# Attention and a gated feed-forward layer on one core: a coarser layout of P, zero rows from DRAM, and new orders

## The chip, the cores and the metric

The kernel runs on one core of one Trainium2 chip. The metric is the device time of that core in microseconds. A run of the kernel takes 270.84 us (median of 7 runs, 266.65 to 271.77).

## The reference

For each of 8 batches and 8 heads, with 576 positions and head size 64, attention with a forget gate is computed; then a feed-forward layer with a convolution over three positions is applied to its output.

```python
scores = scale * np.matmul(q, k.transpose(0, 1, 3, 2))
cum = np.cumsum(np.log(np.clip(f, 0.0001, 1.0)), axis=-1)
scores = np.where(causal, -1e9, scores + cum[:, :, :, None] - cum[:, :, None, :])
attn = softmax(scores)                     # over the keys
x = np.matmul(attn, v)                     # heads side by side: (8, 576, 512)
h = np.maximum(x @ w_in, 0.0)              # 512 -> 1024
conv_out = sum of conv_w[k] * h moved by k - 1 positions, k = 0, 1, 2
out = (h * sigmoid(conv_out)) @ w_out      # 1024 -> 512
```

## The kernel before

**Head blocks.** The 64 heads are worked on in 16 blocks of 4 (`hb`), two blocks for each batch. For a block, q and k come from DRAM by transposing DMAs (`load_qk`, L172) into a tile `qk`. There are four such tiles (`RING = 4`), so a load has to wait until the block four earlier has its scores. A transposed element of 4 bytes fills two partitions, its upper half the odd one, its lower half the even one. The lower halves are not used: the even partitions are given other contents, namely the cumulated logarithms of the gate and constants in a few rows, so that one score matmul adds the decay, and zeros in all the others. For the first six blocks (`NCL = 6`) VectorE does this by multiplying (`clamp`, L182) and GpSimd's DMAs bring the rows. From block 6 on, two DMAs of SyncE do it (`fill`): L203 writes zeros into 60 even partitions, from a row of zeros in SBUF (`cz`) that is read eight times for each partition, and L205 writes the four decay rows from `image`, a tensor in DRAM. `image` is made by GpSimd's DMAs (`decay_image`, `constants`, L209 to L216); its part `image[3]` is all zeros. A fill may start only when both q and k of its block have landed.

**Scores and P.** The scores are computed with keys on the partitions and queries along the columns, for 5 blocks of keys (the last of 64). Because of the causal mask, key block m meets the queries from 128 m on. TensorE computes them in tasks into PSUM tiles `ps` of 1024 columns (four of them): `diag_scores` for two heads (8 squares of 128 by 128 on the diagonal), `off_scores` for one head (the remaining 448, 320, 192 and 64 columns of key blocks 0 to 3), `tail_scores` for the fifth key block of four heads. ScalarE takes the exponentials (`off_exp`, L363, straight into the tile `pp`; `diag_exp`, L375, into `pd`; `tail_exp`, L348), and GpSimd masks the squares on the diagonal on their way from `pd` into `pp` (`diag_mask`, L378), and the tail into `pt` (`tail_mask`, L351).

**Sweeps.** `sweep` (L400) multiplies P by a weight of 32 columns for four heads. The heads go to four strips of 32 columns of the TensorE array. `sums` does it once for a block, with ones; `pv` does it twice, with the even and the odd columns of V. So there are 48 sweeps. Each walks over `PIECES`, ten pieces of P given as key block, first query, number of queries, and kind; each piece is one matmul for each of the four heads. VectorE then makes reciprocals of the sums (`recip`, L408 to L410) and multiplies (`norm`, L417) into `xt`.

**Feed-forward.** For each batch and each of 8 groups of 128 channels: `ffn1` (TensorE, L427), `relu` (ScalarE, L431), `conv` in two halves (VectorE, L437 and L439), `tanh` (ScalarE, L442), `gate` (VectorE, L446). Then `ffn2` (TensorE, L453 and L458; `ffn2_last`, L467 and L470, for the last batch), `evac` (L478, L480) and `store` (L486, L489).

**Order.** Every step is a task in a `Plan`. For each engine a string `ORDER` gives the order of its tasks, one letter for each (`KINDS`): on PE `d`, `o`, `t` are scores, `s` and `p` sweeps, `f` and `g` to `m` the two products of the feed-forward layer; on SP `q` is a load of q or k, `y` of V, `j` and `J` of weights, `z` a fill, `S` a store. Each engine takes its own string strictly in order and waits by semaphores. `Plan.play` uses the times in microseconds that each task is given (estimates, with `lock=True` for steps in which VectorE and GpSimd exclude each other) to merge the strings and to choose buffers; the order within an engine is that of the string. All of SyncE's loads, fills and stores share one DMA queue, in the order of its string.

Of the kernel before, what the change touches and what calls it, by code (L numbers as in the profile page):

```python
# [14 lines left out]
AF = mybir.ActivationFunctionType  # L15
ALU = mybir.AluOpType
# [68 lines left out]
def kernel(  # L85
# [11 lines left out]
    nc = tc.nc  # L97

    B, H, S, D = q.shape
# [10 lines left out]
    HH = 4  # L110
# [3 lines left out]
    WARM = {0: 16, 2: 4, 4: 6, 6: 6}  # L114
    AB = 256
    MB = 224
# [84 lines left out]
    def fill(hb):  # L201
        c = slice(hb * HH, (hb + 1) * HH)
        nc.sync.dma_start(even_rows(hb, 8, 60, 0, 2 * HS).rearrange("p (r x) -> p r x", x=S),  # L203
                          zero[0:60].unsqueeze(1).broadcast_to((60, 2 * HH, S)))
        nc.sync.dma_start(even_rows(hb, 0, 4, 0, 2 * HS).rearrange("j (a x) -> j a x", a=2),  # L205
                          image[:, :, c, :].rearrange("j a h s -> j a (h s)"))
# [147 lines left out]

    OFF = {0: 0, 3: 448, 1: 512, 2: 832}

    def off_scores(me, i, s):
        hb, h = where(i, s)
        for m in (0, 3, 1, 2):
            scores(ps_t[slot[me, "ps"]], OFF[m], hb, h, 128 * m, 128 * (m + 1), S - 128 * (m + 1))  # L360

    def off_exp(t_sc, t_dg, s):
        nc.scalar.activation(pp_t[slot[t_dg, "p"]][:, 1024 * s:1024 * (s + 1)], ps_t[slot[t_sc, "ps"]], AF.Exp,  # L363
                             scale=SCALE)

    def diag_scores(me, i):
        for x in range(WARM.get(i, 0) if i else 0):
            nc.tensor.matmul(ps_t[slot[me, "ps"]][:, 0:512], kc[:, 0:128], kc[:, 64:576], start=True, stop=True)
        for s in range(2):
            hb, h = where(i, s)  # L370
            for m in range(4):
                scores(ps_t[slot[me, "ps"]], 512 * s + 128 * m, hb, h, 128 * m, 128 * m, 128)

# [3 lines left out]
    def diag_mask(t_dg, t_ex):  # L377
        nc.gpsimd.affine_select(pp_t[slot[t_dg, "p"]][:, 2048:3072].rearrange("p (m j) -> p m j", j=128),  # L378
                                pd_t[slot[t_ex, "pd"]].rearrange("p (m j) -> p m j", j=128), pattern=[[0, 8], [1, 128]], base=0, channel_multiplier=-1,
                                compare_op=ALU.is_ge, fill=0.0)  # L380

    PIECES = [(0, 128, 128, "o"), (0, 0, 128, "d"), (1, 128, 128, "d"),
              (0, 256, 320, "o"), (1, 256, 320, "o"), (2, 384, 192, "o"), (3, 512, 64, "o"),
              (2, 256, 128, "d"), (3, 384, 128, "d"), (4, 512, 64, "t")]

    def sweep(ps, hb, t_dgs, t_tail, left_of):

        pt = pt_t[slot[t_tail, "pt"]]
        for x, (m, q0, n, kind) in enumerate(PIECES):
            for h in range(HH):  # L390
                pp, s = pp_t[slot[t_dgs[h // 2], "p"]], h % 2
                if kind == "o":
                    c = 1024 * s + OFF[m] + q0 - 128 * (m + 1)
                    p = pp[:, c:c + n]
                elif kind == "d":
                    c = 2048 + 512 * s + 128 * m
                    p = pp[:, c:c + n]
                else:
                    p = pt[:, SL * h:SL * (h + 1)]
                nc.tensor.matmul(ps[32 * h:32 * (h + 1), AB + q0:AB + q0 + n], left_of(h, m), p,  # L400
                                 start=x in (0, 3), stop=x in (2, 9), skip_group_check=True)

# [103 lines left out]
    for hb in range(NHB):  # L506
        b = hb // 2
        old = [t_exp[x] for x in t_exp if x[0] == hb - RING]
        for s in (1, 0):
            if hb < 2:  # L510
                t_ld[hb, s] = at(13.1 if s else 17.0)
            else:
                t_ld[hb, s] = add("load_qk", "SP", 1.3, old, lambda me, hb=hb, s=s: load_qk(hb, 0, 4, s), dma=2.95)
        if hb % 2 == 0:
            t_vl[b] = add("load_v", "SP", 3.0, [], lambda me, b=b: load_v(b, vf_t[slot[me, "vf"]]), take=["vf"],
                          dma=5.3)
        if hb == 0:
# [40 lines left out]
        for p in range(2):  # L558
            i = 2 * hb + p
            slow = ((3.0, 1.2)[p] if hb < 2 else 1.0)  # L560
            if p == (hb < 2):
                x = t_tail[hb] = add("tail_scores", "PE", (0.5 if hb < 2 else 0.2), rows[0] + rows[1], lambda me, hb=hb: tail_scores(me, hb),
                                     take=["ps", "pt"])
                y = t_exp[hb, "t"] = add("tail_exp", "ACT", 0.31, [x], lambda me, x=x: tail_exp(x, me), take=["p3"],
                                         give=[("ps", x)])
                t_tmask[hb] = add("tail_mask", "POOL", 0.45, [y], lambda me, x=x, y=y: tail_mask(x, y), give=[("p3", y)],
                                  lock=True)
            x = t_dg[i] = add("diag_scores", "PE", 0.46 * slow, rows[p], lambda me, i=i: diag_scores(me, i),
                              take=["ps", "p"])
            y = t_exp[hb, p, "d"] = add("diag_exp", "ACT", 0.94, [x], lambda me, x=x: diag_exp(x, me), take=["pd"],  # L570
                                        give=[("ps", x)])
            t_mask[i] = add("diag_mask", "POOL", 1.12, [y], lambda me, x=x, y=y: diag_mask(x, y), give=[("pd", y)],
                            lock=True)
            for s in range(2):
                z = add("off_scores", "PE", 0.46 * slow, rows[p], lambda me, i=i, s=s: off_scores(me, i, s),
                        take=["ps"])
                t_exp[hb, p, s] = add("off_exp", "ACT", 0.94, [z, x], lambda me, z=z, x=x, s=s: off_exp(z, x, s),
                                      give=[("ps", z)])
# [17 lines left out]
    for b in range(B):  # L596
        for ff in range(NFF):
            ready = [t_norm[4 * b + c] for c in range(4)] + t_win[4:6 if ff < 4 else 8]
            x = add("ffn1", "PE", 0.98, ready, lambda me, b=b, ff=ff: ffn1(me, t_x0[b], ff), take=["ps", "ht"],
                    give=[("xt", t_x0[b])] if ff == NFF - 1 else [])  # L600
            y = add("relu", "ACT", 0.57, [x], lambda me, x=x: relu(x), give=[("ps", x)])
            u0 = add("conv", "DVE", 0.735, [y, t_cwt], lambda me, x=x, ff=ff: conv(x, me, ff, 0), take=["u"], lock=True)
            u1 = add("conv_end", "DVE", 0.735, [u0], lambda me, x=x, u0=u0, ff=ff: conv(x, u0, ff, 1), lock=True)
            if ff == 0:
                th = g0 = add("tanh", "ACT", 0.69, [u1], lambda me, u0=u0, ff=ff: tanh(u0, me, ff), take=["hg"],
                              give=[("u", u0)])
            else:
                th = add("tanh", "ACT", 0.69, [u1], lambda me, u0=u0, g0=g0, ff=ff: tanh(u0, g0, ff), give=[("u", u0)])
            gates[b, ff] = add("gate", "DVE", 0.68, [th], lambda me, x=x, g0=g0, ff=ff: gate(x, g0, ff), give=[("ht", x)],
                               lock=True)  # L610
# [17 lines left out]
        for c in range(5):  # L628
# [6 lines left out]
            if c in (1, 3, 4):  # L635
# [4 lines left out]

    KINDS = {"w": "conv_weights", "d": "diag_scores", "o": "off_scores", "t": "tail_scores", "s": "sums",
             "p": "pv", "f": "ffn1", "g": "ffn2", "h": "ffn2_end", "l": "ffn2_last", "m": "ffn2_last_end",
             "O": "off_exp", "T": "tail_exp", "D": "diag_exp", "c": "cast_in", "R": "relu", "H": "tanh",
             "C": "cast_out", "E": "evac", "e": "evac_end", "k": "clamp", "W": "conv_ratios", "v": "cast_v",
             "V": "cast_v_end", "r": "recip", "n": "norm", "a": "conv", "b": "conv_end", "G": "gate",
             "x": "own_rows", "9": "own_row", "N": "tail_mask", "M": "diag_mask", "i": "decay_image",
             "X": "rows_of", "I": "constants", "y": "load_v", "j": "load_in", "q": "load_qk", "J": "load_out",
             "z": "fill", "S": "store"}
    ORDER = {
        "PE": "wdootdodooosdtopopsppffffdodfofotfofddooostoppdosdopoptffffoggtfdofosgdogpofpstddfpopooohffffgtd"  # L650
              "gfooffsdgotgpodposfdppohoffoffgtdogosggfdfoppoftddosfpopoohffstdfpdfogoopfdgofofogtgsfdopohpdtds"
              "ffppooffgofogfsdtfopgopdfgfohffodfosfgfpdogofptofhsgppgffffgggffhfllgflllllllllllllmmmmlmmmm",
        "ACT": "OOTDDOOODODTOOcRRcRHHRHDDOHRRTORHORODOODOTHCOHDODCCTOHRCRRRHOOHTERDOHROHHODEORHTDDROHOOeHRRROHTR"
               "HDHROORRHDEOHTEHODOHRDOeRHORRORHTODHHHEOERDROHORTDDORHOOOHeRRHTDRDROHOOHDHRERORHOHHTOERDOOeHTDRD"
               "HROORHRHOROHERDTHROHODRHHERHOReHROROHDRHRHODEORTHOHReHHRRRREHHEHRReHHRHREHHEe",
        "DVE": "kWkkkvVvrVncnrnnkababaGbaGcbkGGabaakbGbrGnanrbnnGkGababGaabGabbrGabGnGnarbnnGabGGaabbabGaGbGabra"
               "baGGnbnGrnnabGGaaabbabbrGGGGabnnaGabrnnGbabGaGrbnabGabanGbGaabbaGbGGranbnGranGnabbGaaGbabGbranGa"
               "GbbnaGbGabGaGababGbraaGbnGbnaGbrannGbGGaababbGaGGababGbaGGabbGGE",
        "POOL": "x9NMMiMMNXXNMMXvVMNMvVMMIXNMNvVMvVNMMvVMNNMvVMvMMNvVVMvMNVMvMVMNNMvMvNVVMvMMNVMMvMNV",
        "SP": "yjjqqjjqqqqyJqJJqJyqqqzqqzSSqyzqySqqzSSqyzqSqqzqqzSSqySzyqqSzSqSqzSSSSSSSSSSSS",  # L660
    }
# [33 lines left out]
```

## Time and profile before

| | |
|---|---|
| profiled execution | 270.84 us |
| its span in the trace | 269.1 us |
| PE, busy | 239.8 us (89%) |
| VectorE (DVE), busy | 224.0 us (83%) |
| ScalarE (ACT), busy | 202.2 us (75%) |
| GpSimd (POOL), busy | 85.7 us (32%) |
| score matmuls, L336 | 576, 64.2 us |
| sweeps, L400 | 1280 matmuls with V recorded, 640 with ones |
| diagonal masks, L378 | 32, mean 1255 ns |
| fills, L203 | 10, 540 KB each, 5.2 us from issue to landing |
| DMA packets | 126098, of which 113735 under 512 B |
| bytes moved by DMA | 49.34 MB |

PE is TensorE's matmul side and PEld its weight loads. Matmuls are pipelined, so a busy PE counts time in which one matmul fills the array while another drains. The span runs from the first to the last instruction of the program. The profile infers who ended a wait; where a wait was for several semaphores it names the one that came last by its records. A share of DMA can exceed 1, since packets of several queues can be under way on one engine.

### The profile page before, as it was taken

To read this page: it belongs to the slowest core of one execution; us is meant where nothing else is said; L and a number is where in the kernel's file an instruction comes from. 1 tells how busy PE (TensorE), PEld (TensorE's weight loads), DVE (VectorE), ACT (ScalarE), POOL (GpSimd) and SP (SyncE) were. 2 spreads that over 40 slices of the span, in tenths; PEclk is the share of its full clock that TensorE was granted. 3 is DMA by queue.
4 is the path that set the end of the run, shared out by engine and by line. 5 is a ranking of instruction groups with operands and counts; after the bars stand their busy time and mean duration, and the time that the engine had idled before them with its cause. 6 is when DMAs were issued, how large, how long until landed. Compare 5 with 4: busy or idle time off the path is not lost.

```text
span 269.1 us, 8203 instructions
## 1 busy us (share of the span) xinstructions
PE 239.8 (89%) x3501; PEld 159.5 (59%) x3504; DVE 224.0 (83%) x327; ACT 202.2 (75%) x272; POOL 85.7 (32%) x113
## 2 busy tenths in 40 slices
PE   7599697967999999999995979998989969999992
PEld 2367465654665776676564656666656646665640
DVE  5645789999989999997786699996998949999871
ACT  4069358996899899988884878996978948928651
POOL 4157111696216701490332504065302103200000
PEclk9989989997999999999998999999999979999999
DMA  6999999999999999989999999999989450202124
GB/s 141 200 231 242 243 200 190 238 287 251 202 197 183 243 217 216 217 169 189 229 220 164 197 177 260 213 200 205 198 222 166 93 197 0 80 2 100 78 97 177
DMA packets 126098, 49.34 MB, mean 183 GB/s; under 512 B 113735, under 2 KB 119571, under 8 KB 126062
## 3 DMA queue, kind: packets, MB, share of 16 engines
q1 hardware_dynamic: 125278, 48.00, 87.6%
q0 software_dynamic: 704, 0.67, 0.9%
q8 instruction: 27, 0.44, 0.7%
q10 hardware_dynamic: 80, 0.15, 0.2%
q14 instruction: 9, 0.07, 0.1%
HBM read 14.36 MB, written 10.03 MB: 91 GB/s over the span
## 4 chain that ended last, share of the span: by engine, by line
PE 45%; DMA 22%; SPq 10%; DVE 10%; ACT 5%; issue 5%; POOL 1%; DVEq 0%; ACTq 0%; POOLq 0%
PE ps L427 12%; PE ps L453 11%; DMA qk<-in_q_dram 10%; PE ps L336 8%; PE ps L400 7%; DMA qk<-image 7%; SPq L172 4%; PE ps L467 3%; SPq L247 3%; DVE u L437 3%; DMA qk<-cz 2%; DMA vf<-in_v_dram 2%; SPq L489 2%; DVE u L439 2%; ACT pp L363 2%
## 5 line engine op out<-in xcount | busy, mean ns | idle before, releaser
L336 PE MATMUL ps<-qk 128*128 128x128 bf16 (+3 forms) x576 | 64.2, 249 | 14.0 <-DMA qk<-image 5.4
L363 ACT ACTIVATE pp<-ps 128x1024 f16<-128x1024 f32 x64 | 65.2, 1032 | 14.0 <-PE ps L341 9.3
L427 PE MATMUL ps<-xt,w_in_f 128*128 128x288 f16 x512 | 72.5, 292 | 1.0 <-DVE xt L417 0.6
L378 POOL TENSOR_SCALAR_AFFINE_SELECT pp<-pd 128x1024 f16<-128x1024 f32 x32 | 40.0, 1255 | 76.9 <-ACT pd L375 76.8
L437 DVE SCALAR_TENSOR_TENSOR u<-ht,cwt 128x576 f32<-128x576 f16 x64 | 54.8, 864 | 7.0 <-ACT ht L431 6.8
L427 PEld LDWEIGHTS <-w_in_f 128*128 128x128 f16 x512 | 49.4, 100 | 17.0 <-issue 1.9
L336 PEld LDWEIGHTS <-qk 128*128 128x128 bf16 x576 | 39.0, 101 | 30.9 <-issue 13.9
L439 DVE SCALAR_TENSOR_TENSOR u<-ht,cwt,u 128x576 f32<-128x576 f16 x64 | 56.6, 895 | 0.6
L431 ACT ACTIVATE ht<-ps 128x576 f16<-128x576 f32 x64 | 41.6, 658 | 18.3 <-PE ps L427 17.7
L442 ACT ACTIVATE hg<-u,cw 128x576 f16<-128x576 f32 x64 | 49.2, 782 | 7.9 <-DVE u L439 7.6
L446 DVE SCALAR_TENSOR_TENSOR hg<-hg,ht 128x576 f16<-128x576 f16 x64 | 50.7, 801 | 3.2 <-ACT hg L442 2.9
L453 PE MATMUL ps<-w_out_f,hg 128*128 128x512 f16 x224 | 52.3, 379 | 0.0
L375 ACT ACTIVATE pd<-ps 128x1024 f32<-128x1024 f32 x32 | 32.5, 1029 | 5.1 <-PE ps L336 4.9
L453 PEld LDWEIGHTS <-hg 128*128 128x128 f16 x224 | 21.1, 98 | 22.0
L400 PE MATMUL ps<-pp,va 128*32 128x128 f16 (+3 forms) x1152 | 27.3, 243 | 2.4 <-issue 2.0
L417 DVE TENSOR_TENSOR xt<-ps,rb 128x576 f16<-128x576 f32 x32 | 24.0, 752 | 6.5 <-PE ps L400 4.6
L400 PEld LDWEIGHTS <-va 128*32 128x32 f16 x1280 | 22.1, 99 | 10.9 <-issue 8.6
L253 POOL CAST va<-vf 128x1024 f16<-128x1024 f32 x14 | 16.6, 1186 | 15.5 <-DMA vf<-in_v_dram 13.9
L478 ACT COPY ob<-ps 128x1024 f32<-128x1024 f32 (+1 forms) x23 | 18.2, 793 | 4.2 <-PE ps L467 1.9
L408 DVE STREAM_TRANSPOSE st<-ps 128x576 f32<-128x576 f32 x16 | 12.4, 777 | 8.3 <-PE ps L400 8.3
L351 POOL TENSOR_SCALAR_AFFINE_SELECT pt<-p 128x256 f16<-128x256 f32 x16 | 9.7, 604 | 19.5 <-ACT p L348 19.5
L400 PE MATMUL ps<-pp,ones_h 128*32 128x128 f16 (+3 forms) x576 | 13.9, 240 | 2.2 <-DVE xt L417 1.6
(87 smaller groups left out, 162.7 us busy)
## 6 DMA issues: line engine op xcount, KB each, us to landing
vf<-in_v_dram SPq DMA_DIRECT2D x32, 256.0 KB, 5.6
out_dram<-ob SPq DMA_DIRECT2D x16, 512.0 KB, 3.9
qk<-cz SPq DMA_DIRECT2D x10, 540.0 KB, 5.2
ob<-in_moe_w_out_dram SPq DMA_DIRECT2D x4, 512.0 KB, 4.8
vf<-in_v_dram SPq DMA_DIRECT2D x8, 128.0 KB, 5.8
vf<-in_moe_w_in_dram SPq DMA_DIRECT2D x2, 512.0 KB
hg<-in_moe_w_in_dram SPq DMA_DIRECT2D x2, 512.0 KB
out_dram<-ob SPq DMA_DIRECT2D x16, 64.0 KB, 3.4
```

What stands on the lines that cost most here:

```text
L336: nc.tensor.matmul(o, tk[:, h * S + k0:h * S + k0 + 128], tq[:, h * S + q0:h * S + q0 + n], start=True, stop=not apart(hb, h))
L363: nc.scalar.activation(pp_t[slot[t_dg, "p"]][:, 1024 * s:1024 * (s + 1)], ps_t[slot[t_sc, "ps"]], AF.Exp, scale=SCALE)
L375: nc.scalar.activation(pd_t[slot[me, "pd"]], ps_t[slot[t_dg, "ps"]], AF.Exp, scale=SCALE)
L378: nc.gpsimd.affine_select(pp_t[slot[t_dg, "p"]][:, 2048:3072].rearrange("p (m j) -> p m j", j=128), pd_t[slot[t_ex, "pd"]].rearrange("p (m ...
L400: nc.tensor.matmul(ps[32 * h:32 * (h + 1), AB + q0:AB + q0 + n], left_of(h, m), p, start=x in (0, 3), stop=x in (2, 9), skip_group_check=True)
L427: nc.tensor.matmul(ps[:, MB + 288 * a:MB + 288 * (a + 1)], w_in_f16[:, cc, 128 * ff:128 * (ff + 1)], xt[:, cc, 288 * a:288 * (a + 1)], sta ...
L431: nc.scalar.activation(ht_t[slot[t_m1, "ht"]][:, 1:1 + S], ps_t[slot[t_m1, "ps"]][:, MB:MB + S], AF.Relu, scale=0.5)
L437: nc.vector.scalar_tensor_tensor(u, ht[:, 0:S], cwt[:, ff, 0:1], ht[:, 1:1 + S], op0=ALU.mult, op1=ALU.add)
L439: nc.vector.scalar_tensor_tensor(u, ht[:, 2:2 + S], cwt[:, ff, 1:2], u, op0=ALU.mult, op1=ALU.add)
L442: nc.scalar.activation(hg_t[slot[t_g0, "hg"]][:, ff, :], u_t[slot[t_u, "u"]], AF.Tanh, scale=cw[:, ff, 1:2])
L446: nc.vector.scalar_tensor_tensor(hv, hv, 1.0, ht_t[slot[t_m1, "ht"]][:, 1:1 + S], op0=ALU.add, op1=ALU.mult)
L453: nc.tensor.matmul(o, hg[:, ff, 128 * c:128 * (c + 1)], w_out_f16[:, ff, :], start=(ff == 0), stop=(ff == NFF - 1))
```

## The change

`pp` gets another layout. Up to now a head's four off-diagonal runs lay together and the squares of both heads behind them. In the new tile the square of key block 1 stands just ahead of the off-diagonal run of key block 1, and the square of key block 3 just ahead of the run of key block 3 (64 queries), so that each pair is one piece. A pass then has 7 pieces. The results of a sweep start at column 384 of the PSUM tile in place of 256 (`AB`), [...]a run of 448 columns is then one piece too. `off_exp` writes two runs of 512 columns, and `diag_mask` becomes two instructions for four squares each, one into the places beside the runs and one into the end of the tile.

The zero rows of a fill come from `image[3]` in DRAM, 9216 contiguous bytes for each partition. Their issue, L203 before, is the same single DMA of SyncE.

Some of the plan's times are raised (the conv halves from 0.735 to 0.79, the exponentials from 0.94 to 0.97, the mask from 1.12 to 1.35, the load of q or k from 2.95 to 3.2 of DMA time, V from 5.3 to 5.7), and all five order strings are new; of these PE's and SP's are shown.

```diff
-    AB = 256
+    AB = 384
...
     def fill(hb):
         c = slice(hb * HH, (hb + 1) * HH)
-        nc.sync.dma_start(even_rows(hb, 8, 60, 0, 2 * HS).rearrange("p (r x) -> p r x", x=S),
-                          zero[0:60].unsqueeze(1).broadcast_to((60, 2 * HH, S)))
+        none = image[3]
+        nothing = bass.AP(tensor=none.tensor, offset=int(none.offset), ap=[[2 * S, 60], [1, 2 * HS]])
+        nc.sync.dma_start(even_rows(hb, 8, 60, 0, 2 * HS),
+                          nothing)
...
-    OFF = {0: 0, 3: 448, 1: 512, 2: 832}
+    OFF = {3: 0, 0: 64, 1: 512, 2: 832}
+    DIAG = (3, 1, 0, 2)
+    AT = {"d3": 0, "o3": 128, "o0": 192, "d1": 640, "o1": 768, "o2": 1088, "d0": 2560, "d2": 2688}
...
+    def blocks(t_dg):
+        return pp_t[slot[t_dg, "p"]][:, 0:2560].rearrange("p (a c) -> p a c", c=640)
+
     def off_exp(t_sc, t_dg, s):
-        nc.scalar.activation(pp_t[slot[t_dg, "p"]][:, 1024 * s:1024 * (s + 1)], ps_t[slot[t_sc, "ps"]], AF.Exp,
+        nc.scalar.activation(blocks(t_dg)[:, 2 * s:2 * s + 2, 128:640],
+                             ps_t[slot[t_sc, "ps"]].rearrange("p (a c) -> p a c", a=2), AF.Exp,
                              scale=SCALE)
...
     def diag_mask(t_dg, t_ex):
-        nc.gpsimd.affine_select(pp_t[slot[t_dg, "p"]][:, 2048:3072].rearrange("p (m j) -> p m j", j=128),
-                                pd_t[slot[t_ex, "pd"]].rearrange("p (m j) -> p m j", j=128), pattern=[[0, 8], [1, 128]], base=0, channel_multiplier=-1,
-                                compare_op=ALU.is_ge, fill=0.0)
-
-    PIECES = [(0, 128, 128, "o"), (0, 0, 128, "d"), (1, 128, 128, "d"),
-              (0, 256, 320, "o"), (1, 256, 320, "o"), (2, 384, 192, "o"), (3, 512, 64, "o"),
-              (2, 256, 128, "d"), (3, 384, 128, "d"), (4, 512, 64, "t")]
+        pd = pd_t[slot[t_ex, "pd"]].rearrange("p (x m j) -> p x m j", x=2, m=4)
+        for x in range(2):
+            to = pp_t[slot[t_dg, "p"]][:, 2560:3072].rearrange("p (m j) -> p m j", m=4) if x else blocks(t_dg)[:, :, 0:128]
+            nc.gpsimd.affine_select(to, pd[:, x], pattern=[[0, 4], [1, 128]], base=0, channel_multiplier=-1,
+                                    compare_op=ALU.is_ge, fill=0.0)
+
+    PIECES = [(0, 0, 128, "d0"), (0, 128, 448, "o0"), (1, 128, 448, "d1"), (3, 384, 192, "d3"), (2, 384, 192, "o2"),
+              (2, 256, 128, "d2"), (4, 512, 64, "t")]
...
     ORDER = {
-        "PE": "wdootdodooosdtopopsppffffdodfofotfofddooostoppdosdopoptffffoggtfdofosgdogpofpstddfpopooohffffgtd"
-              "gfooffsdgotgpodposfdppohoffoffgtdogosggfdfoppoftddosfpopoohffstdfpdfogoopfdgofofogtgsfdopohpdtds"
-              "ffppooffgofogfsdtfopgopdfgfohffodfosfgfpdogofptofhsgppgffffgggffhfllgflllllllllllllmmmmlmmmm",
+        "PE": "dootdoowdosotdopopsppffffdtfodfoofoddofotosodoppdosotppffffgogstfdogdgoopfpofsdotofdppohftofdfgd"
+              "fofogffosofdpopotsdpgoopgfdtffohofdogfsogpdfsofftoggpdoppodffhtdfsoofogffpdgtoofsogdfopopdgpdofs"
+              "hffotofgopdgfpofffdogstoogpdpshfofdpoffotpfoggsfpfpgfghfffgfhgffgflgllfllllllllllllmmmmlmmmm",
...
-        "SP": "yjjqqjjqqqqyJqJJqJyqqqzqqzSSqyzqySqqzSSqyzqSqqzqqzSSqySzyqqSzSqSqzSSSSSSSSSSSS",
+        "SP": "yqjjqjjqqqqyJJqJqJyqqqzqqzqqSyzqSyzqSqSzzqqyzqSqqzSqqzySqSzqqyzSSSSSSSSSSSSSS",
```

The scores of the diagonal are written in the order `DIAG` for both heads, and the score tasks and the sweep follow the new places (`OFF`, `AT`); their counts and sizes stay the same.

## The prediction

> **What bounds the kernel now.** I read the slices of the span first (rows are engines, one digit for each 6.7 us).
>
> ```profile
> PE   7599697967999999999995979998989969999992
> DVE  5645789999989999997786699996998949999871
> PEclk9989989997999999999998999999999979999999
> DMA  6999999999999999989999999999989450202124
> ```
>
> Two rows are full together: PE, and, up to slice 31 (about 215 us), the DMA engines. Behind that point the DMA row falls to 0 to 4 while PE stays full, so PE sets the end of the kernel and DMA decides when PE may go on before that. The list of waits, for PE from 69 us on, says where it could not:
>
> ```profile
> PE ps L336 <- DMA qk<-image: 5.4, 4, 2.3
> PE ps L336 <- DVE u L439: 3.1, 1, 3.1
> PE ps L336 <- DMA qk<-cz: 1.0, 1, 1.0
> ```
>
> All three are the first score matmul of a head block (L336) waiting for its q/k tile. The middle one names DVE, but the wait ends at 145.5 us, 1.1 us after the last packet of the tile's rows from `image` (144.4 us in the trace's DMA packets); the wait at 217.4 us ends 1.2 us after its last such packet. It is a DMA wait too. Sum: 5.4 + 3.1 + 1.0 = **9.5 us**. The chain of waits shows one of them whole (start, length, what):
>
> ```profile
> 204.93 6.31 DMA qk<-in_q_dram
> 211.29 0.97 SPq L203
> 212.31 4.82 DMA qk<-image
> 217.13 0.24 issue
> 217.37 1.01 PE ps L336 x8
> ```
>
> q lands; only then may SP issue the fill (L203, zero rows; then L205, the four decay rows), and 6 us later PE starts. The view by windows (length, busy time of PE, PEld, DVE, ACT, POOL, granted PE clock, DMA share, GB/s) prices it:
>
> ```profile
> 70.00:100.00 30.00, 30.00 (x453) 20.59 (x451) 28.26 (x39) 28.13 (x40) 11.75 (x13) 1.00 1.07 203
> 213.00:215.90 2.90, 2.06 (x18) 1.40 (x15) 2.87 (x5) 2.62 (x6) 0.00 (x0) 1.00 0.90 228
> 217.30:220.00 2.70, 2.63 (x16) 2.00 (x17) 0.28 (x1) 0.00 (x0) 0.00 (x0) 0.50 0.64 211
> ```
>
> Without a DMA wait PE is busy 30.00 of 30 us (first row). The fill keeps the DMA engines for some 3 us (second row). After the wait the clock is 0.50 (third row): a window of 3.4 us at half rate, also seen at 145.4 us, each costing 1.7 us. So DMA waits cost 9.5 + 2 x 1.7 = **12.9 us**.
>
> **The change, part by part.** The sums start from the profiled execution, 270.84 us (span 269.1 and 1.7 around it), which is also the median of the seven runs.
>
> *Seven pieces for ten.* 48 sweeps lose 3 pieces of 4 heads each, 576 matmuls with their weight loads; the columns stay 1600 for each head. One sweep after another:
>
> ```profile
> 139.35 0.85 PE L400 MATMUL ps<-pp,va 128*32 128x128 f16 x36
> 140.05 0.84 PE L400 MATMUL ps<-pp,va 128*32 128x128 f16 x36
> ```
>
> 40 matmuls (36 and the 4 of the tail) start 0.70 us ahead of the next 40. ffn2's matmuls of 512 columns take 1.73 us for 8, so 0.42 ns a column, and 1600 columns alone are 0.675 us. Ten pieces thus cost some 0.025 us beyond their columns, 2.5 ns each, because the four heads stream side by side; 48 x 3 x 2.5 ns = **-0.4 us**. The Trainium skill ("TensorE: Matmul & The Clock Gate", "Wait — 56ns, not 53.3ns?") would give far more: warm matmuls never start closer than about 25 ns, so 576 fewer are 14.4 us. Here 0.70 us / 40 is 17.5 ns already, below that floor, so I take the row. Bounds: 0 and -0.4; one issue stall of 2.0 us in a V sweep at 30 us, where PE waited for nothing shown, and the half-rate window behind it (1.7) could go with the instructions: -3.7, kept for the range.
>
> *Zero rows from DRAM.* Ten fills of 553 KB, each now 480 packets of 1152 B. The packets' median is 81 ns, and from the first to the last packet a fill takes 3.0 to 4.0 us, mean 3.3. The new fill has 60 packets of 9216 B, 4 in a row for the busiest of 16 engines. The trace has none; the nearest row is the DRAM packet of 4608 B (`image` rows): median 178 ns, mean 211 in mixed traffic. Twice that is 356 to 423 ns, four are 1.4 to 1.7 us: a fill is shorter by 1.6 to 1.9 us. From the other side, the largest packets seen, 16384 B of instructions, took a median of 1072 ns (15 B/ns): 603 ns x 4 = 2.4 us, shorter by 0.9. I take **1.6 us**, by the nearest row. A rule of the Trainium skill speaks against this part: its page "DMA: Bandwidth & Descriptors" says ("Why small descriptors are slow (HBM only)") that SBUF-to-SBUF transfers do not suffer from small packets, and ("Where 436 GB/s comes from") that they are bound at 435 GB/s where HBM transfers are bound at 358. By that a fill of 553 KB goes from 1.27 to 1.54 us, and ten lose 2.7 us. The packets decide: 553 KB in 3.0 us (212.9 to 215.9 us) is 184 GB/s, so this SBUF-to-SBUF copy is slow. The four rows of L205 stay as they are. The new source needs `image` written, which POOL does far ahead (L214 to L216 at 65 us, first fill at 80).
>
> *The orders.* Counted in PE work (ffn1 0.98, ffn2 1.73, scores 0.45, sweep 0.70 us by the chain's rows), the new PE order reaches the first scores of block 9, 10, 11, 13, 14 and 15 earlier by 5.7, 6.1, 3.7, 3.4, 5.1 and 4.7 us; block 12 at the same place. The new SP order (3.3 us for a q or k load, 5.5 for V, 1.3 for a store) puts the fills of 9, 10, 11, 13, 14 and 15 earlier by 4.6, 5.5, 4.6, 4.8, 5.5 and 2.6 us; that of 12 at the same place. So the order asks for rows earlier than it brings them, and the fills must make up the rest. From block 9 at 128.0 us, at 1.04 us for each unit of work (13.5 us for 13.0 between blocks 9 and 10), with the k-th fill gaining k x 1.6 us:
>
> | block | PE asks (us) | rows there (us) | least gain for each fill (us) |
> |---|---|---|---|
> | 10 | 135.2 | 145.5 - 5.5 - 8.0 = 132.0 | 1.0 |
> | 12 | 160.6 | 167.9 - 11.2 = 156.7 | 1.0 |
> | 14 | 185.5 | 200.9 - 5.5 - 14.4 = 181.0 | 1.1 |
> | 15 | 200.1 | 217.4 - 2.6 - 16.0 = 198.8 | 1.5 |
>
> Blocks 9, 11 and 13 have more room. At 1.6 us no wait remains: **-12.9 us**. That the gains add up rests on the DMA engines never being out of work: between 70 and 205 us the packets leave no gap over 0.9 us. What is late next is DVE.
>
> *Two masks for one.* POOL's 32 selects of 1024 columns become 64 of 512.
>
> ```profile
> L378 POOL TENSOR_SCALAR_AFFINE_SELECT pp<-pd 128x1024 f16<-128x1024 f32 x32 | 40.0, 1255 | 76.9 <-ACT pd L375 76.8
> L351 POOL TENSOR_SCALAR_AFFINE_SELECT pt<-p 128x256 f16<-128x256 f32 x16 | 9.7, 604 | 19.5 <-ACT p L348 19.5
> ```
>
> Undisturbed ones took 1092 and 419 ns, so 512 columns are 643 ns by the line through both, and a mask takes 0.19 us longer: 6.2 us of POOL in all. POOL idles 76.9 us before these, so its own time is hidden; the sweep behind a mask gets it 0.2 us later, and the order has other PE work there. But DVE's conv and gate instructions (median 751 to 812 ns) took 1018 to 1194 where they overlap POOL, 12 us too many in all. In proportion to POOL's time (62 us) that grows by 1.2; by its count (76 instructions, 0.16 each) by 5. DVE has 28.26 of 30 us filled where PE never waits, so I charge it to the path: **+3 us**, between the two. Bounds: -1 (a shorter select holds DVE up less) and +5.
>
> *The rest.* Exponentials write two runs of 512 instead of one of 1024; no row shows that, the reads and their count are the same: 0, with +0.05 x 64 = 3 us as the far end (ACT idles 14 us before them). The first w_in halves come behind a k load in the new SP order, up to 3.3 us later; ffn1 starts at 33.6 us after PE itself is late: 0, at worst +3.3. The constants of conv move behind the first scores: 0.7 us of PE, moved only.
>
> Sum: 270.84 - 0.4 - 12.9 + 3 = 260.5 us.
>
> **The rivals.**
>
> *The long packets gain nothing.* They are cut up again, or DRAM delivers at the rate of the old copy; this is also "it does not do what it says". For it: the rule above. Against it: the 4608 B packets. Block 15 is then asked for at 200.1 and there at 214.8 us, 14.7 late, where the old order is 12.4 late by the same count: 2.3 us slower, **273 us**. In between, at 0.9 us for each fill, block 15 is 14.7 - 9 = 5.7 us late: 260.5 + 5.7 = 266.
>
> *DVE becomes the bound.* Place: the conv and gate instructions between 70 and 217 us; mechanism: each added select holds up a DVE instruction for its whole length, 32 x 0.64 = 20.6 us. For it: DVE already fills 94% of the stage that runs free, and single conv instructions took up to 3.3 us beside POOL. Against it: 150 of 192 conv and gate instructions met no POOL work. DVE's 224 + 20.6 us at 94% are 260 us, with 13 at the start and 5 at the end 278: **278 us**, slower. It decides from about 14 us of added DVE time, where 238 / 0.94 + 18 = 271.
>
> **How the numbers follow.** The likeliest case gets 0.62: 260.5 us. Its own range is 254 (the issue stall gone too, no DVE cost) to 266. No gain from the packets, 0.24, at 266 to 273; DVE as the bound, 0.14, at 271 to 280. The range 254 to 273 leaves out most of the last and a little below. Two per cent, about what a measurement of this kernel can tell from no change, is 265.4 to 276.3 us: 0.62 faster, 0.24 same, 0.14 slower.
>
> **What would show it.** Right: fill packets of 9216 B at 360 to 420 ns, a fill in 1.4 to 1.7 us, PE's waits for q/k tiles after 69 us below 2 us, no half-rate window after 69 us, the DMA row falling some 10 us sooner; a sweep 0.68 us. Wrong: waits for `image` still near 9 us (first rival), or PE waiting for DVE with DVE above 240 us busy (second). A gain in the sweeps of many us would prove me wrong on the pieces.

## The result, and the profile after

The changed kernel takes **266.17 us** (median of 27 runs, 263.05 to 270.91), the kernel before 270.21 us beside it. The ratio is 0.9859, 95% interval 0.9831 to 0.9886: faster by 1.4%, so within the 2% that I called no change. I forecast 260.5 us and gave "faster by over 2%" 0.62. The profiled execution took 267.47 us with a span of 265.7, so it is 7.0 us longer than forecast. The intermediate case of the first rival (0.9 us for each fill, 266 us) comes closest. Executions of one kernel differ by up to 4%: a median here counts all of them, a ratio only the undisturbed ones, so that it need not be the quotient of the medians beside it, and as the changed kernel's own trace is of a slow one, that of e17 stands beside it.

The slices of the span, of the changed kernel (each digit 6.6 us):

```profile
PE   7599975759899999999999999999889889999992
DVE  5632999974999998989998879997959999889971
PEclk9779999997999999999999999999999999999997
DMA  6999999999996999999999989999999510202224
```

DMA's full stretch ends less than a slice sooner (5 and 1 in slices 31 and 32, counted from 0, where it had 4 and 5), and not the 10 us forecast; the last fill's last packet is there at 207.1 us, before at 216.0. Behind slice 9 the clock row stays at 9: the half-rate windows at 145 and 217 us are gone. PE stands at 8 in slices 31 and 32, just where DMA becomes idle. The list of waits of PE from 69 us on, of the changed kernel (total us, times, longest):

```profile
PE ps L338 <- DMA qk<-image: 2.5, 2, 1.7
PE ps L406 <- DVE xt L423: 1.2, 1, 1.2
PE ps L433 <- ACT ht L437: 0.8, 2, 0.5
PE ps L338 <- ACT pd L383: 0.6, 1, 0.6
PE ps L406 <- ACT ht L437: 0.5, 2, 0.3
PE ps L433 <- ACT pd L383: 0.3, 1, 0.3
...
```

Before, there were six waits, all for q/k tiles, of up to 3.1 us and 9.5 us in sum. Now those for q/k tiles come to 2.5 us. In their place PE waits for ACT and DVE, 4.7 us in twelve short waits (the rows left out included), which before it did not.

I counted the loss of PE by stage: the time at which PE reaches a point in its order, less the PE work that the order has ahead of that point (by the durations used in the prediction). All loss is in us; the two kernels in italics are experiments below.

| loss of PE | up to block 6's scores | from there to block 15's scores | after that | in all |
|---|---|---|---|---|
| before | 39.0 | 16.8 | 2.9 | 58.7 |
| changed | 40.3 | 10.9 | 4.3 | 55.5 |
| *changed again (e17)* | 42.0 | 11.5 | 4.3 | 57.8 |
| *layout and fill, old orders (e5)* | 38.8 | 12.7 | 1.4 | 52.9 |

The forecast was 16.8 - 12.9 + 3 - 0.4 = 6.5 in the middle stage and nothing elsewhere. So 4.4 us of the 7.1 missing ones are in the middle, 1.3 at the start, 1.4 at the end.

One caution on ratios. The layout alone came out at 0.9755 on one chip (from three runs) and at 0.9913 on another (from ten). Kernels of different groups of runs are therefore compared only to about 1.5%; where I need less, both ran on the same chip, and their ratio is that of the medians of the runs that a ratio counts, with a 95% interval from resampling them.

### The profile page after: what moved, and what is told of

Its sections match the earlier page's. It is cut to its first block, busy times and chain, and to the rows that moved or that the text cites. A ratio compares the mean times of both kernels' runs of the same rounds, so it can differ in the third digit from the quotient of the medians.

```text
span 265.7 us, 7090 instructions
## 1 busy us (share of the span) xinstructions
PE 238.7 (90%) x2925; PEld 154.8 (58%) x2928; DVE 222.0 (84%) x327; ACT 202.5 (76%) x272; POOL 91.7 (35%) x145
## 4 chain that ended last, share of the span: by engine, by line
PE 53%; ACT 14%; DMA 13%; SPq 10%; issue 5%; DVE 2%; POOL 0%; ACTq 0%; POOLq 0%; DVEq 0%
PE ps L433 16%; PE ps L459 15%; PE ps L338 9%; PE ps L406 7%; DMA qk<-image 6%; DMA qk<-in_q_dram 6%; SPq L172 6%; ACT pp L370 5%; ACT pd L383 3%; SPq L249 3%; PE ps L473 3%; ACT hg L448 2%; ACT ht L437 2%; PE ps L464 2%; ACT w_out_f L243 1%
## 5 line engine op out<-in xcount | busy, mean ns | idle before, releaser
L433 PE MATMUL ps<-xt,w_in_f 128*128 128x288 f16 x512 | 71.2, 286 | 4.0 <-DVE xt L423 1.9
L338 PE MATMUL ps<-qk 128*128 128x128 bf16 (+2 forms) x576 | 63.5, 244 | 10.5 <-DMA qk<-image 4.8
L389 POOL TENSOR_SCALAR_AFFINE_SELECT pp<-pd 128x512 f16<-128x512 f32 x64 | 47.7, 769 | 47.9 <-ACT pd L383 46.1
L443 DVE SCALAR_TENSOR_TENSOR u<-ht,cwt 128x576 f32<-128x576 f16 x64 | 55.9, 880 | 7.3 <-ACT ht L437 7.0
L452 DVE SCALAR_TENSOR_TENSOR hg<-hg,ht 128x576 f16<-128x576 f16 x64 | 49.4, 784 | 1.5 <-ACT hg L448 1.2
L423 DVE TENSOR_TENSOR xt<-ps,rb 128x576 f16<-128x576 f32 x32 | 23.7, 750 | 5.9 <-PE ps L406 5.3
L406 PE MATMUL ps<-pp,va 128*32 128x128 f16 (+2 forms) x768 | 27.6, 281 | 1.1 <-ACT ht L437 0.5
L406 PEld LDWEIGHTS <-va 128*32 128x32 f16 x896 | 19.2, 99 | 12.1 <-issue 6.1
L353 POOL TENSOR_SCALAR_AFFINE_SELECT pt<-p 128x256 f16<-128x256 f32 x16 | 8.0, 499 | 39.2 <-ACT p L350 24.9
L255 POOL CAST va<-vf 128x1024 f16<-128x1024 f32 x14 | 15.4, 1107 | 16.7 <-DMA vf<-in_v_dram 16.7
L406 PE MATMUL ps<-pp,ones_h 128*32 128x128 f16 (+2 forms) x384 | 13.7, 274 | 2.0 <-DVE xt L423 1.2
```

Source lines behind the costliest of these rows:

```text
L338: nc.tensor.matmul(o, tk[:, h * S + k0:h * S + k0 + 128], tq[:, h * S + q0:h * S + q0 + n], start=True, stop=not apart(hb, h))
L389: nc.gpsimd.affine_select(to, pd[:, x], pattern=[[0, 4], [1, 128]], base=0, channel_multiplier=-1, compare_op=ALU.is_ge, fill=0.0)
L433: nc.tensor.matmul(ps[:, MB + 288 * a:MB + 288 * (a + 1)], w_in_f16[:, cc, 128 * ff:128 * (ff + 1)], xt[:, cc, 288 * a:288 * (a + 1)], sta ...
L443: nc.vector.scalar_tensor_tensor(u, ht[:, 0:S], cwt[:, ff, 0:1], ht[:, 1:1 + S], op0=ALU.mult, op1=ALU.add)
L452: nc.vector.scalar_tensor_tensor(hv, hv, 1.0, ht_t[slot[t_m1, "ht"]][:, 1:1 + S], op0=ALU.add, op1=ALU.mult)
```

## The experiments: one part at a time

The first six combine the three parts of the change: layout (seven pieces, two masks), fill (zero rows from DRAM), orders (with the planned times).

**e1, the layout alone.** `OFF`, `PIECES`, `AT`, `AB`, the exponentials and masks as in the changed kernel; fill, ORDER and planned times as before.

> Old orders and old fill, new layout of P alone (7 pieces, two masks for one, results from column 384). Theory (the layout is worth next to nothing either way): a sweep gets 7 ns shorter, 48 of them 0.3 us; masks are 0.18 us later, hidden: 268.5 to 271 us, within 0.5% of before. Rival (the added selects hold DVE up): 1.2 to 5 us slower, 271.5 to 275 us, with DVE's conv and gate instructions above the 12 us of excess that before shows.

268.29 us, ratio 0.9755 (0.9681 to 0.9829). The layout is worth more than the 0.3 us of the expectation. PE's stall near 30 us is gone (below).

**e2, the fill alone.**

```diff
-        nc.sync.dma_start(even_rows(hb, 8, 60, 0, 2 * HS).rearrange("p (r x) -> p r x", x=S),
-                          zero[0:60].unsqueeze(1).broadcast_to((60, 2 * HH, S)))
+        nc.sync.dma_start(even_rows(hb, 8, 60, 0, 2 * HS), nothing)
```

> Old orders and old layout, zero rows from DRAM in packets of 9216 B alone. Theory (the kernel is held up by DMA in front of the late blocks, and a fill of 2.65 us for 3.15 gives back 0.5 us each time): rows of block 15 some 5 us earlier, waits of PE for q/k tiles 9.5 us down to 4 to 5, time 264.5 to 267 us. Rival (what the fills give is lost to waits on ACT and DVE): 268.5 to 270.5 us, with the waits for q/k tiles as far down but as much added in front of ACT and DVE.

269.29 us, ratio 0.9885 (0.9834 to 0.9935): a gain of 3.1 us. Neither expectation holds: PE still waits 4.3 us for rows of `image`, and once 2.4 us more at the same instruction, named for DVE, so 6.7 us and not 4 to 5; no waits for ACT came in after 69 us; and the rows of block 15 are there 1.6 us sooner (last packet at 214.7 us, before at 216.3), not 5.

**e3, the orders and planned times alone.**

> New orders and plan times alone, with the old layout and the old fill. Theory by the count of the prediction (the new order asks for blocks 9 to 15 earlier than it brings their rows): 2.3 us slower than before, 271.5 to 273.5 us, with waits for q/k tiles of 9 us or more. Rival (the orders are the gain of the changed kernel): 265 to 267.5 us, as the changed kernel or nearly.

272.59 us, ratio 1.0066 (1.0022 to 1.0111): slower, as expected, but not by the expected waits: after 69 us PE waits 3.5 us for rows, less than before. By the count of the table above it loses 3.3 us more than before up to block 6's scores (its stall near 30 us is 3.3 us, before 2.0), 2.6 us less from there to block 15's, and 1.0 us more after that.

**e4, fill and orders on the old layout.**

> New orders and new fill, old layout. If the layout is worth next to nothing this is the changed kernel's time, 265 to 267.5 us. If the two masks for one cost the changed kernel time, this is faster than it by 1.2 to 5 us, 261 to 265 us.

269.37 us, ratio 0.9872 (0.9823 to 0.9922), above both expectations. On the same chip that is 0.9865 (0.980 to 0.989) of the orders alone, so here the fill again brings some 3.7 us; and 0.9985 (0.993 to 1.006) of the fill alone, so the orders bring nothing. In its trace PE waits only 0.6 us for `image` after 69 us (e2: 4.3, or 6.7 with the wait named for DVE). The waits for rows are gone and the time is unchanged: against e2, it loses 5.6 us less between block 6's and block 15's scores, but 3.9 more ahead of them, where its stalls with no semaphore to wait for come to 5.4 us (e2: 1.9), and 2.5 more behind them.

**e5, layout and fill with the old orders.**

> Old orders with the new layout and the new fill. If the layout (ratio 0.9755 alone) and the fill (0.9885 alone) act on different losses, the layout on PE's issue stall near 30 us and the fill on the waits for q/k tiles, their gains add up: ratio 0.964, some 261 to 264 us, faster than the changed kernel. Rival (both act on one loss, and the changed kernel shows all there is): 0.975 to 0.986, 265 to 268 us.

266.79 us, ratio 0.9813 (0.9761 to 0.9866), in the range of the rival; but the theory's 0.964 rested on e1's 0.9755, and with the later 0.9913 for the layout (e15) the sum of the gains is 0.980. Its waits of PE from 69 us on:

```profile
PE ps L338 <- DMA qk<-image: 4.5, 3, 2.9
PE ps L338 <- DVE xt L423: 0.7, 2, 0.5
```

More DMA waiting than in the changed kernel (4.5 against 2.5 us), next to no waiting for ACT and DVE, and no more time in all.

**e6, layout and orders with the old fill.**

> New layout and new orders, old fill. If the parts are independent: 0.9755 x 1.0066 = 0.982. Theory (the new orders ask earlier and need the faster fill more than the old ones do): waits for q/k tiles of 5 us or more and a ratio of 0.985 to 0.995. Rival (the fill does not matter under the new orders): as the changed kernel, 0.986 or less, with the same short waits on ACT and DVE.

272.64 us, ratio 0.9984 (0.9939 to 1.0029), slower than both expectations: with the old fill, the new orders leave nothing of what the layout brought alone. e5 on the same chip is 0.9825 of it (0.977 to 0.991).

**e7 and e8: where the layout's gain sits.** Both are e1 with the layout kept, but the sweeps cut into ten pieces again: e7 all 48 sweeps, e8 only the six of head blocks 0 and 1.

```diff
+    CUT = {"o0": (128, 320), "d1": (128, 320), "d3": (128, 64)}
...
-        for x, (m, q0, n, kind) in enumerate(PIECES):
+        pieces = TEN if True else PIECES        # e8: if hb < 2
+        for x, (m, q0, n, kind, at) in enumerate(pieces):
```

> The kernel of e1_layout (old orders, old fill, new layout and masks), but every sweep cut into ten pieces again: the same columns, the same data, the same masks, only 576 matmuls and as many weight loads more on PE. Theory (PE runs out of fetched instructions in the first burst of sweeps): the stall of about 2 us near 30 us, in which PE waits for nothing shown, is back, with a half-rate window behind it, and the time is 4 to 6 us over e1_layout, ratio to before 0.99 to 1.00. Rival (the gain of the layout lies in its banks, its masks or in chance): the time stays at e1_layout's, ratio 0.97 to 0.98.

> As e7_ten_pieces, but only the six sweeps of head blocks 0 and 1 are cut into ten pieces, the other 42 keep seven. Theory (what counts is the burst of sweeps near 30 us): the stall is back, and most of the loss with it, ratio 0.985 to 1.00. Rival (the gain comes from 7 ns and fewer fetches in all sweeps): ratio 0.97 to 0.98, no stall near 30 us.

272.12 us, ratio 0.9976 (0.9929 to 1.0022), and 271.62 us, ratio 0.9972 (0.9925 to 1.0020). Ten pieces take away the layout's gain, and ten in six sweeps of 48 do it as well. These six follow each other near 30 us. The timeline of PE there, of e7 (start, length, instructions, in brackets the idle time before and its releaser):

```profile
30.76 0.47 PE L412 MATMUL ps<-pp,va 128*32 128x128 f16 x13
32.48 0.54 PE L412 MATMUL ps<-pp,va 128*32 128x320 f16 x20 [1.26 <-issue]
```

Thirteen matmuls into a sweep PE stops for 1.26 us, and no semaphore is waited for. That is the stall of 2.0 us that the prediction saw in the kernel before; e8 has it with 2.1 us, e1 does not. A transfer of instructions (a DMA packet of 16384 B) begins about then, but so it does, at 28.7 to 31.7 us, in the kernels that do not stall. Two other things point to it. All eight kernels that stall here (before, e2, e3, e4, e7, e8, e12, e18) stop ahead of the same matmul, the 348th or 349th recorded; and each time PE goes on 1.35 to 1.58 us after the end of that transfer, however long it stood (0.5 to 3.4 us). I read it as PE running out of fetched instructions; no run changed the supply of instructions by itself. e1 was on another chip than these two, so the size of the gain lies between 0.9% (e15) and 2.4% (e1).

## The experiments: the fill and the DMA engines

**e9, zero rows from rows of their own.** The changed kernel; the source is a DRAM tile of 60 distinct rows instead of overlapping ranges of `image[3]`. It is written once at the start (one DMA more, 576 KB).

```diff
+    empty = dpool.tile([64, 2 * HS], BF16, name="empty")
...
-        nc.sync.dma_start(even_rows(hb, 8, 60, 0, 2 * HS), nothing)
+        nc.sync.dma_start(even_rows(hb, 8, 60, 0, 2 * HS), empty[0:60])
```

> The changed kernel, its zero rows read from a DRAM tensor of their own with 9216 different bytes for each of the 60 rows (GpSimd writes it once, 590 KB, with the constants), where the changed kernel's rows overlap within 147 KB. In the changed kernel 15 packets are under way together and take 600 ns, where single ones took 347. Theory (the overlapping rows crowd one part of DRAM): packets of 350 to 450 ns, a fill in 1.5 to 1.9 us for 2.65, some 262 to 264 us. Rival (the limit lies on the way into SBUF or in the engines): packets of 600 ns, a fill of 2.5 to 2.8 us, time as the changed kernel, 265 to 268 us.

272.97 us, ratio 1.0067 (0.9996 to 1.0139). The packets of 9216 B keep a mean of 594 ns (600 in the changed kernel): that many rows are read from the same place is not what makes them long. The kernel is slower, by 1.3% (0.3 to 1.6) also than e10 on the same chip. Its least disturbed fills last 3.0 to 3.4 us, in the changed kernel 2.6 to 3.0, and it has the added write; which of the two costs the time is not settled.

**e10, the fill in packets of 2304 B**, four times as many.

> The changed kernel, its zero rows read from the same place in packets of 2304 B, four for each row, all from the row's first 2304 bytes. Theory (length does not matter any more once the packets come from DRAM): a fill of 2.5 to 2.8 us and the time of the changed kernel. Rival (long packets are what helps): 240 packets take 3.0 us or more for a fill, and the time is 1 to 3 us over the changed kernel's.

269.76 us, ratio 0.998 (0.992 to 1.004). The packets of the fills take 147 ns in the mean, in sum 22.1 us on each of the 16 engines; the long ones of the changed kernel come to 22.5, the old ones of 1152 B to 24.8. From 2304 B to 9216 B the length of the packet does not matter to DMA's work. Whether it matters to the time is open: the changed kernel (0.986 to 0.991 elsewhere) was not run on this chip.

**e11 and e12: less for DMA to do.** The V loads of batches 4 and 6 are left out, some 11 us of DMA time, in the changed kernel (e11) and in the kernel before (e12).

```diff
+        if b in (4, 6):
+            return
```

> The changed kernel without the V loads of batches 4 and 6, whose blocks use the V of earlier batches: some 11 us of DMA work less before the last blocks, about what the prediction had the ten fills give beyond the measured 0.5 us each. Theory (the fill's size was the term that failed, and DMA decides): waits for q/k tiles after 69 us gone, 259 to 262 us. Rival (the new order keeps PE waiting on ACT and DVE whatever DMA does): 264 to 266 us, with the short waits on ACT and DVE, some 5 us in all, still there.

> The kernel before without the same two V loads: 11 us of DMA work less under the old orders and layout. Theory (DMA waits and their half-rate windows, 12.9 us, go when DMA has 11 us less to do): 258 to 262 us. Rival (most of it turns into waits on ACT and DVE, or DMA is held back by its ring of four tiles): 265 to 269 us. The issue stall near 30 us stays in both.

266.80 us, ratio 0.9873 (0.9815 to 0.9932), and 264.0 us, ratio 0.9766 (0.9641 to 0.9892). In the kernel before, some 6.3 us come back, between theory and rival (four runs). Its trace keeps one row of waits after 69 us, and one of two half-rate windows:

```profile
PE ps L338 <- DMA qk<-cz: 5.1, 3, 2.7
```

e11 looked no faster than the changed kernel, but had run on another chip; of e10, on its own chip, it is 0.990 (0.985 to 0.995). So the next four ran together.

**e13 to e16, on one chip:** the changed kernel, layout and fill with the old orders, the layout alone, the changed kernel with fewer V loads.

> The changed kernel itself, beside three others on one chip, because the runs so far were compared only through the kernel before and on different chips. Theory (the new orders give the freed DMA time away to waits for ACT and DVE): it is 0.5 to 1% slower than the layout and the fill with the old orders, and no slower than itself with fewer V loads. Rival (the differences are those between chips): ratio to before 0.98 to 0.99, and all four kernels of this call within 0.5% of each other.

> The new layout and the new fill with the orders and planned times of before, as in e5. Theory: ratio to before 0.975 to 0.982, 0.5 to 1% below the changed kernel of this call; PE waits for q/k rows (4 to 5 us) in its trace and hardly for ACT or DVE. Rival (new orders cost nothing): equal to the changed kernel within 0.3%.

> The new layout alone, as in e1. If the fill's gain adds to the layout's: 1.0% slower than the layout with the fill. If it doesn't (the fill's 0.5 us for each block is taken up by other transfers when PE runs ahead): within 0.4% of it.

> The changed kernel without the V loads of batches 4 and 6 (that part of the computation is left out), as in e11, now beside the changed kernel. Theory (DMA no longer sets the time under the new orders): equal to the changed kernel within 0.4%. Rival (DMA still does): 1% or more, some 3 us, faster than the changed kernel; then e11's ratio of 0.9873 was that of another chip.

| kernel | median, us | ratio to before | against the changed kernel |
|---|---|---|---|
| e13 changed | 268.92 | 0.9914 (0.9849 to 0.9978) | |
| e14 layout, fill | 265.41 | 0.9789 (0.9693 to 0.9886) | 0.986 (0.977 to 0.994) |
| e15 layout | 269.50 | 0.9913 (0.9870 to 0.9956) | 1.001 (0.998 to 1.009) |
| e16 changed, less V | 266.39 | 0.9831 (0.9751 to 0.9910) | 0.989 (0.986 to 0.997) |

Four readings. The orders cost 1.4%, some 3.7 us, once layout and fill are in, in the direction of the theory (it said 0.5 to 1%). The fill on top of the layout brings 0.985 (0.975 to 0.990), some 4.0 us, so their gains add up. Fill and orders together bring nothing here: the changed kernel cannot be told from the layout alone. And less DMA work still brings 1.1%, 2.5 to 3 us, as the rival had it; the interval begins at 0.3%, so by itself this is weak against the theory that DMA no longer sets the time, but e11 against e10 says the same. It is about half of what the same cut brings before the change.

**e17 and e18: is the stall's end worth anything in the changed kernel?** e17 is the changed kernel, e18 the same with ten pieces in the six early sweeps, as in e8.

> The changed kernel once more, as the partner of the next run on the same chip. Both theories: ratio to before 0.985 to 0.992, and no stall named issue of over 1 us before 40 us in its trace.

> The changed kernel, with ten pieces instead of seven only in the six sweeps of head blocks 0 and 1 (144 matmuls more in 1600, of 7 ns for each sweep, 0.04 us, by the time of the isolated sweep). Theory (PE runs out of fetched instructions near 30 us where many sweeps follow each other, and the layout's gain is that this goes): a stall named issue of 2 to 4 us near 30 us, and 2 to 4 us (0.8 to 1.5%) slower than its partner. Rival (under the new orders the stall is cover for transfers that PE would wait for anyway): the stall is seen, and the time stays within 0.4% of its partner's.

268.83 us, ratio 0.9864 (0.9799 to 0.9929), and 270.13 us, ratio 0.9881 (0.9832 to 0.9930); e18 is 0.996 (0.991 to 1.008) of e17. (The six sweeps have 72 matmuls and 72 weight loads more.) Both sides missed: the stall hardly came, as this row of the waits of PE from 15 to 69 us in e18 shows, and the time stayed.

```profile
PE ps L414 <- issue: 0.5, 1, 0.5
```

So ten pieces alone do not bring a long stall; it also matters when PE gets to the place. In e18 the transfer of instructions had ended at 31.02 us, 0.95 us before PE stopped; in e8 it ended at 30.82, 0.57 us after. e4, with ten pieces everywhere under the new orders, stalls for 3.4 us there and for 2.0 us at 66 us (again until 1.5 us after such a transfer), yet its ratio, from another chip, is no worse than that of the changed kernel. Under the new orders no gain of the layout was seen.

## What the new orders give and take

The three stages of the table on PE's loss tell it. In the middle one, where DMA is full, the new orders lose less than the old ones with the same layout and fill: 10.9 and 11.5 us in two executions against 12.7. Up to block 6's scores they lose more: 40.3 and 42.0 against 38.8. After block 15's scores they lose 4.3 in both, and 4.2 in e4, against 1.4 in e5, e14, e15 and e2: some 2.9 us, the same in every kernel with these orders. The view by windows (length, busy time of PE, PEld, DVE, ACT, POOL, granted clock, DMA share, GB/s), first e5, then the changed kernel:

```profile
130.00:160.00 30.00, 26.21 (x373) 17.39 (x374) 23.98 (x34) 24.02 (x33) 10.73 (x16) 0.96 1.04 211
208.00:240.00 32.00, 32.00 (x384) 20.89 (x383) 31.55 (x45) 25.22 (x38) 6.40 (x8) 1.00 0.21 69
```

```profile
130.00:160.00 30.00, 28.86 (x397) 18.73 (x392) 26.33 (x37) 25.23 (x36) 10.86 (x16) 1.00 1.09 215
190.00:215.00 25.00, 22.10 (x313) 14.42 (x311) 21.73 (x29) 18.29 (x24) 8.63 (x13) 1.00 0.85 202
208.00:240.00 32.00, 29.89 (x403) 19.98 (x392) 29.71 (x41) 21.94 (x32) 5.70 (x9) 1.00 0.15 55
```

From 130 to 160 us the new orders are ahead by 2.65 us of PE work. From 208 to 240 us, DMA's share is 0.15: nothing is waiting for rows. With the old orders PE is busy 32.00 of 32 us there; with the new ones 29.89, and e17 has the same 29.89. The timeline of PE shows the largest hole, of the changed kernel:

```profile
208.68 0.84 PE L406 MATMUL ps<-pp,va 128*32 128x128 f16 x24
209.35 0.20 PE L406 MATMUL ps<-pt,va 128*32 128x64 f16 x4
210.72 0.84 PE L406 MATMUL ps<-pp,ones_h 128*32 128x128 f16 x24 [1.17 <-DVE xt L423]
...
215.88 0.84 PE L406 MATMUL ps<-pp,va 128*32 128x128 f16 x24 [0.35 <-ACT ht L437]
...
217.71 2.12 PE L433 MATMUL ps<-xt,w_in_f 128*128 128x288 f16 x16 [0.32 <-ACT pd L383]
```

The chain of waits says what the sums sweep at 210.72 waits for (start, length, what):

```profile
208.75 0.83 PE ps L406 x28
209.58 0.03 issue
...
209.93 0.74 DVE xt L423
```

The new order puts the sums sweep right behind a V sweep. It needs a PSUM tile that is free only when DVE has normalised (L423) the V sweep that has just ended: 0.83 us of sweep, 0.74 of DVE, and what lies between, with no PE work to fill it. Then single sweeps and ffn1 come just ahead of the ACT instruction that frees theirs. A faster fill can't help here. What costs up to 3 us ahead of block 6 is not settled: the named waits there differ between executions (w_out's cast by ACT, rows of `image`, a k load). The order of one engine with the old ones of the others was not tried.

## Why the prediction was wrong, point by point

- **The failed step is the term of -12.9 us, in two parts: the fill was mis-sized, and the orders were put at 0.** On one chip (e13 to e15) the fill on the layout brought 4.0 us and the orders took 3.7 of them back. The layout with its masks, forecast at -0.4 + 3, brought 2.4 us there, so an error the other way hid a part of it.
- **The fill.** I put a packet of 9216 B at twice one of 4608 B, 356 to 423 ns. It takes 599.5 ns in the median (345 at least), and the 4608 B packets of the rows behind it rise from 178 to 334 ns in the median too. The bound from the 16384 B packets, 603 ns, was right; I had set it aside for the nearer row, whose 178 ns came from transfers of eight packets. A fill with little other traffic lasts 2.65 us instead of 3.15: **0.5 us** gained, not 1.6. (In e2 two such fills took 3.7 us, so not every one gains.)
- **The table of rows fell with it.** The last packets of the rows of blocks 10, 12, 14 and 15 are there at 136.9, 165.2, 192.0 and 207.1 us. With the 1 us or so from there to PE's start, which the table's times include, that is about 6, 9.5, 12 and 9.3 us later than I had them; 1.1 us missing in each fill makes 5.5, 7.7, 9.9 and 11. So gains add up from fill to fill, roughly. PE's waits for the rows came to no more than 2.5 us only because PE itself came later: it asked for block 15 at 208.1 us and not at 200.1.
- **The orders were put at 0 beyond the rows.** They cost 1.4% beside layout and fill; by the table of PE's loss, 2.9 us after block 15's scores. I had taken an order that asks 3 to 6 us sooner as a gain once the rows are there, and not asked whether ACT and DVE can free the tiles as much sooner. DVE filled 94% of the free-running stage, which I had used only for the masks.
- **The DMA waits counted fully only under the old orders.** In e12 the waits for rows fall from 9.5 to 5.1 us and the half-rate windows of 1.7 us from two to one, 6.1 us by the prediction's count, and some 6.3 us come back. In the changed kernel they fall by 7.0 us and both windows are gone, as forecast, 10.4 us by that count, and 3.8 come back: most of the difference is 4.7 us of waits for ACT and DVE and 1.3 more lost ahead of block 6. So the fill at its forecast size would probably not have been enough: another 11 us off DMA brings the changed kernel 2.5 to 3 us (e16).
- **The pieces: right on the sweep, wrong on the kernel, and cancelled.** A sweep by itself went from 807 to 800 ns from its start to the next instruction's, so 48 sweeps give 0.34 us (forecast 0.4), and the row of 17.5 ns a matmul was the right one against the floor of 25 ns of the Trainium skill ("TensorE: Matmul & The Clock Gate", "Wait — 56ns, not 53.3ns?"), which would have made 14.4 us. But under the old orders the layout brings 0.9 to 2.4%, most likely through the early stall that I kept for the range; under the new orders no gain of it was seen.
- **Masks right, their cost not there.** This row of the costliest groups of the changed kernel has 64 selects:

```profile
L389 POOL TENSOR_SCALAR_AFFINE_SELECT pp<-pd 128x512 f16<-128x512 f32 x64 | 47.7, 769 | 47.9 <-ACT pd L383 46.1
```

  Undisturbed ones take 635 ns (forecast 643), and the group grows by 7.7 us (40.0 before; forecast 6.2). The 3 us of DVE did not come: DVE's busy time is 222.0 us against 224.0. So the second rival, DVE as the bound through the selects, was wrong; DVE does hold PE up now, but through the orders.
- **Rival one** (long packets gain nothing) was nearly right on the rate, 15 against 14 B/ns on a DMA engine, and wrong on the time: the fill alone brings 1.15%, 3.1 us. The rule that it rested on (the Trainium skill, "DMA: Bandwidth & Descriptors", "Why small descriptors are slow (HBM only)": a copy inside SBUF does not suffer from small packets) would have lost 2.7 us by the prediction's estimate. The case between, 0.9 us a fill and 266 us, has the right time for partly other reasons: a smaller gain of the fill, and a loss from the orders.

## A version faster than both

Layout and fill with the old orders (e5, e14): ratios to before 0.9813 and 0.9789, and 0.986 (0.977 to 0.994) of the changed kernel on one chip. The intervals of the two ratios to before reach from 0.969 to 0.989, so whether it is faster than before by 2% is open.

## What to carry to other kernels

Where an instruction order is searched for a faster transfer, look at what the other engines must free by then: an engine 94% full can give back as waits what the transfer has won. Take a packet's time from packets that run as many together as the new ones will, not from the nearest size. And measure the parts of a change beside each other on one chip, since here the same kernel's ratio to a common partner moved by 1.5% between chips.

## What the runs showed of the hardware

- Packets of a fill, of 1152 B from SBUF, and of 2304 and 9216 B from DRAM, took 83, 147 and 600 ns in the mean: 14, 16 and 15 B/ns on a DMA engine. From 2304 to 9216 B the length bought nothing, and leaving SBUF for DRAM lost nothing.
- A 9216 B packet took 345 ns at the fastest and 600 in the median, with some 14 under way together (60 packets of 600 ns in 2.65 us).
- PE stood still for 1.3 to 3.4 us near 30 us with no semaphore to wait for, in e2, e3, e4, e7, e8, e12 and the kernel before, where up to 40 matmuls of a sweep follow each other within 0.7 us. It went on 1.35 to 1.58 us after a transfer of 16384 B of instructions had ended; in e18, where that transfer ended earlier than PE got there, it stood for 0.5 us.
